# Landmark attention and an MLP on one core: the first weight matrix is cast on its way in, and the gain of the norm moves elsewhere

## The chip, the core and the metric

One core of a Trainium2 chip runs the kernel. TensorE (PE) multiplies matrices into PSUM; VectorE (DVE) and ScalarE (ACT) read PSUM and write SBUF; GpSimd (POOL) works from SBUF to SBUF; SyncE (SP) only starts transfers, which POOL and ACT also do, each from its own queue. 16 DMA engines, shared by all queues, move the data. The metric is device microseconds of one execution: the median of three runs of the kernel before is 260.62 us (260.29 to 260.78).

## The reference

Attention runs over batch 8, 8 heads, sequence 576, head dimension 64, with 32 landmarks: means of 18 rows of q or k. Three softmax matrices are formed, A from q and the landmarks of k, B from both kinds of landmarks, C from the landmarks of q and k. Z is an approximate inverse of B, found by six steps. Then follows a layer norm with gain `g_ln` and a two-layer MLP:

```
Z = B^T / (norm1(B) * norminf(B));  six times: Z = 2 Z - Z B Z
x = A Z C v                          # heads side by side: 576 x 512 for each batch
xn = (x - mean(x)) / std(x) * g_ln
out = x + relu(xn @ w_ch1) @ w_ch2   # w_ch1 is 512 x 2048, w_ch2 is 2048 x 512
```

## The kernel before, in words

The rows of x enter the MLP only through a short product. With Zc = Z C v (32 rows for each head), x is A times Zc, so `relu(xn @ W1)` is made from a small matrix m16 = Zc W1 (`psm`, then `m16`), and from A^T, kept as `ea`: `psh = m16^T ea`, `relu` writes `hT`, and W2 is applied to `hT`. The factor 1/std is positive and is applied at the very end, as `rstd`.

**W1, g and the mean.** `load_w1_0` to `load_w1_7`, all on SP, bring W1 as fp32 in eight pieces of 512 KB into the six staging buffers `stg`, which first hold q, k and v of batch 0; a piece waits until the cast that reads the buffer's former content is done. 16 operations `scale_w1_*` on POOL and ACT multiply by 16 g, row by row, and write the fp16 matrix `w1_16`. It has four column quarters f = 0 to 3. `less_mean_f*` (PE) multiplies a quarter by the constant matrix `lesser`, -1/512 everywhere; the result `less_f` is minus the column mean. For batches 0 and 1 the mean is taken off in `m16`: DVE computes less * zsum + psm. For the later batches `center_f*`, eight operations on DVE, adds `less_f` to W1 itself, so that `m16` is a plain copy. `zt_0` and `zt_1` are the transposed Zc of batches 0 and 1, copied from PSUM by `ztc_00`, `ztc_01` and `ztc_1`.

**W2.** It arrives as fp16 by four casting transfers on POOL's queue. Batches 0 and 1 use it plainly (`pso`); from batch 2 on, a scheme with seven half products takes the place of eight (`ps7a`, `ps7c`, `ps7e`) and uses differences of parts of W2 (`mix`) and of `hT` (`hmix`), made by POOL and DVE.

**Batches.** Batch 0 is loaded as fp32 by SP and cast by three engines; its transposes are made on PE (`turns_*`) and copied out of PSUM by `turned_*`. For the others q and k come as fp16 by casting transfers on POOL's queue into three buffers `nat`, v by SP into two buffers `vs`. Batch 1 is worked alone, batches 2 and 3, 4 and 5, 6 and 7 in pairs. The six steps are `step_*` (PE) and `next_*` (DVE or ACT) in turn. In the head of the kernel the chain is: cast of q and k, sums for the landmarks (`sums_*`), `qbd` and `klm`, `psb_0`, `expb_0`, `softmax_0`, `gram_*`, `scaled_0`, six steps, `zt_*`, `ztc_*`, `psm_01` (quarter 1 is taken first), `m16_01*`, `psh_0*`.

**The order.** There is no planner in the kernel: `ORDER` is a list of 1571 entries, a number and an engine letter each (P TensorE, D VectorE, A ScalarE, G GpSimd, S SyncE). The number names an operation, the letter the engine that does it. Every engine works through its own entries in this order, so one operation that waits holds back all that follow on its engine, transfers that this engine starts included. The first W1 piece stands seventh on SP after the loads of q, k and v. `warm_*` are 15 groups of matmuls on zeros whose results nobody reads.

Lines: 193 is every ordinary matmul, 197 the PE transposes, 200 copies and casts, 203 activations, 207 sums of two tensors, 210 the three-operand form, 223 every transfer, 357 the scaling of W1 on POOL, 1068 a relu on DVE, 1202 the making of g.

Of the kernel before, what the change touches and what calls it, by code (L numbers as in the profile page):

```python
# [19 lines left out]
0G 20P 23P 4S 12P 14P 24P 17P 11P 2S 1S 3S 6S 7S 10P 21P 28G 38P 25A 26D 34P 39D 40P 29P 30A 31P 27D  # L20
37P 32P 42D 41D 18P 33D 43P 65P 44A 45D 66A 61P 67P 46P 47P 250G 48D 22P 19P 15P 62A 68A 69A 71D
245G 49P 50D 63P 35P 13P 79G 80D 51P 52D 64A 36A 81P 70D 53P 72P 73A 5S 95S 54D 8P 9D 105A 106G 55P
56D 57P 74P 82D 260P 83D 58D 16P 84D 96S 59P 75A 76A 60D 85P 251D 86D 89P 90D 87P 88D 126P 261A 262D
108G 77G 94S 103G 93S 97S 101G 91D 92D 78D 107A 102G 127P 128P 129P 130A 167P 141P 142A 252P 253A
145P 169D 104A 168D 98S 254D 149P 150D 147P 148A 172P 173A 176P 247P 177A 248A 259D 255D 174P 175A
246D 256P 257A 146A 170P 171D 109G 110G 121P 122P 123P 111G 124P 268P 156P 258D 151D 249D 267P 112A
125A 275A 269A 270A 271A 157D 277A 158D 131P 132P 133P 134P 178P 163P 278D 279D 117G 273A 433G 274A
99S 113G 135A 180D 263S 164A 159P 280P 281D 160A 165P 166A 114G 264A 100S 115G 116G 265S 118G 136P
137P 266G 161P 179D 429G 119G 138P 139P 162D 282P 283D 140A 181P 182A 183P 284P 276D 285A 143P 187P
184D 286P 144A 188A 272D 152D 185P 186A 287D 297P 298D 299D 189P 191D 190D 288P 289A 294P 290P 295A  # L30
201P 202P 296A 300P 301A 291D 292P 293A 120G 455G 212P 213P 435G 436G 437G 310P 438G 445G 302A 303G
308P 309A 214P 330P 434D 444D 312D 311D 313D 332D 192P 193A 153D 154D 198P 199A 155A 441D 430D 439D
431D 331D 442D 440D 432D 443D 234P 556D 215P 304P 235P 236P 305A 306A 196P 446G 447G 203P 204P 194P
195A 237P 238P 205P 206P 451G 197A 307G 314P 315A 337P 339P 448G 449D 822G 338A 555D 239P 240P 241P
322P 207P 208P 574D 565D 569G 450D 340A 323A 216P 242D 209D 210S 217P 324D 341P 343D 223P 335P 244S
336A 342D 333P 463D 218P 219P 577G 452D 220D 344P 352P 353D 467G 468G 469G 470G 334A 826G 348P 345A
349A 346P 347A 457G 318P 319A 224P 316P 317A 225P 226P 227P 481P 458G 465D 459G 460G 482A 350P 454D
354D 357P 471D 464D 472D 351A 453D 363P 228P 229P 364D 358A 361P 230P 362A 461D 462D 365D 493P 494A
359P 368P 360A 483P 495P 355P 325D 326D 505A 369A 356A 231D 233A 200G 374P 375P 366P 367A 370P 371A
573G 506D 456D 507P 508P 509D 320P 321D 385P 484P 486A 487A 489A 510P 834D 511D 466D 491A 386P 387P  # L40
485A 388P 211S 512P 376P 473S 474G 490A 377P 496P 498A 501A 499A 497A 513D 514P 327D 488D 492D 328D
396P 397P 475S 476G 566G 828G 829G 830G 831G 572G 477S 478G 838G 839G 844G 564G 568G 503A 378P 379P
380P 515D 823D 502A 221S 504D 372P 516P 479S 480A 500D 517D 836D 528P 529P 530D 531D 398P 399P 373A
381P 522P 518P 389P 329A 866S 382D 418P 519D 824D 559D 520P 521D 523A 532P 419P 420P 524A 533A 534A
558D 550P 551D 552D 553D 548P 549A 421P 422P 423P 536P 424P 425P 848G 535G 832D 833D 554D 232S 867A
537A 538A 539G 560D 525P 527A 400P 401P 557D 426D 427S 605P 526A 606A 840G 841G 594P 595A 561D 540P
541A 390P 391P 611P 612A 837D 596D 827D 392P 393D 825D 850G 851G 852G 563D 603P 604A 853G 562D 859D
842D 860G 861G 843D 579P 613P 614A 407P 580A 601P 602A 609P 610A 1217G 585P 408P 845D 599P 409P 607P
600A 410P 411P 586A 597P 608A 542A 543G 856D 615P 598A 576G 626P 616A 412P 413P 581P 627A 402P 862G
394S 582A 570G 567D 617D 589D 835D 863G 858D 590D 618P 619A 634P 635A 643P 583P 584A 620P 621A 624P  # L50
414P 571G 874P 625A 622P 623A 628P 629A 644P 544P 847D 857D 545A 846D 591D 546A 875D 403P 632P 872S
633A 645P 630P 647P 592D 631A 646P 415D 877P 648P 649P 650P 864D 865D 854D 404D 855D 1191G 886P 638D
637G 641G 663P 664P 665P 639D 640D 662G 428S 417S 406S 661D 593A 882A 884A 879A 880A 883A 652D 878A
651D 657D 887A 889P 892A 896A 658D 666P 668D 894A 895A 849D 667D 653P 654P 711P 722P 712A 723A 891A
890A 655P 656P 547G 575G 675P 676P 677P 728P 729A 678P 695P 696A 1192D 713D 716P 881D 1194D 717A
724P 725A 876P 888P 1213G 660D 587P 870S 714P 416S 659D 871G 873G 384S 1229G 642G 1230G 1231G 726P
898A 715A 679D 682D 669P 897D 727A 588A 730P 222S 1232G 899D 900P 901P 731A 718P 732P 902D 743P 719D
578G 903P 904D 670P 720P 734A 733A 721D 744A 671P 672P 673D 699P 700A 893D 739P 636G 1203D 1239S
701P 905P 243S 741P 906D 740A 751P 674D 742A 703P 752A 907P 735P 736A 737P 383S 868S 681S 680S 683S
738A 702D 908D 909P 1219G 1195G 1220G 1221G 685P 704D 697P 698A 915P 917A 916A 910D 911P 1222G 759P  # L60
760P 749P 811P 925P 750A 761P 885D 869G 921P 926A 927A 753G 922P 1225D 755G 912D 913P 705D 706D 745P
746A 1227D 812P 707D 708D 709D 710A 813P 814P 747P 748A 686P 687P 688P 928G 929P 930A 1223D 1224D
1196D 1233D 815P 816P 923D 1228D 924D 914D 931A 1214D 943P 947D 944D 941P 817P 946D 945D 1240G 754G
756G 932G 758G 942A 762P 692D 767D 694S 689D 818P 763P 764P 918P 765P 766P 395S 1241S 1197G 920A
1198G 1199G 1200G 919A 819D 963P 974P 965A 975A 1207G 1208G 1209G 768D 769P 964D 774D 770P 956P 968P
1215D 1204D 957A 966P 690S 693S 405S 773D 969A 1226D 779P 967A 933P 934A 935A 780P 972P 948P 949A
1234D 1216D 970P 781P 973A 936G 984P 985A 820S 771P 971D 757D 986D 980P 772P 978P 782P 954P 776D
1242A 775D 981A 979A 976P 977A 955A 937P 1193D 938A 939A 1205D 785P 786P 787P 788P 982P 983A 1255P
989P 990A 1210G 684S 783D 1211D 1212D 1201D 1202D 1243P 777G 778G 784D 790D 691S 991P 1244A 789D
992A 801P 1235S 995P 996A 1245P 940G 1236G 1256D 1257P 802P 1267A 1268D 987P 988A 803P 993P 994A  # L70
1066P 1067D 804P 808D 1269P 1270P 1237S 1238G 1246P 1249A 805D 791P 792P 810S 1206D 1271D 821S 1248A
1247A 1253A 1250D 1251A 793P 958D 794P 1006G 1252A 809S 1003P 1004A 1272P 798D 1273D 997P 998A 950P
# [36 lines left out]
def kernel(  # L109
# [61 lines left out]
    def T(name):  # L171
        return handles[name]
# [1091 lines left out]
```

## Time and profile before

| | |
|---|---|
| median of three runs | 260.62 us |
| the profiled execution | 260.2 us, span 258.5 us |
| PE, DVE, ACT, POOL busy | 249.9, 212.3, 163.9, 177.5 us |
| read from HBM, written | 36.70 MB, 9.44 MB |

The span runs from the first to the last instruction; 1.7 us of the profiled execution's time lie around it. Busy PE is the time in which at least one matmul is in flight. Matmuls overlap, so that a row of eight with one duration may have been stretched by short waits that are no idle time. The granted TensorE clock was full in every part of the span.

### The profile page before, as it was taken

The page shows a single profiled execution, that of the slowest core. Times are in us where ns is not written, and L with a number is a line of the kernel's source. Part 1 is how long each engine was busy: PE and PEld are TensorE (multiplying, and loading weights), DVE is VectorE, ACT ScalarE, POOL GpSimd, SP SyncE. Part 2 cuts the span into 40 slices and gives each one's busy share as a digit, 9 for nine tenths or more (in the row PEclk, how much of TensorE's full clock was granted, in tenths as well). Part 3 has the DMA queues.
Part 4 walks back from the last instruction along what each step waited for, and adds up shares of the span by engine and source line. Part 5 has one row for each costly group of instructions (what it writes and reads, how often), then busy time and mean ns, then how long its engine had stood idle before and what let it go on. Part 6 is the DMA issues. An engine that isn't in the chain of part 4 may idle for free.

```text
span 258.5 us, 8351 instructions
## 1 busy us (share of the span) xinstructions
PE 249.9 (97%) x3499; PEld 179.8 (70%) x3499; DVE 212.3 (82%) x472; ACT 163.9 (63%) x304; POOL 177.5 (69%) x180
## 2 busy tenths in 40 slices
PE   7898999999999999999999999999999999999993
PEld 7766465556554557777766787777867787788981
DVE  1669899999999989997998869898547999878661
ACT  1588886747766999778756997868666245644000
POOL 8324899689794789699999995782078505966600
PEclk9999999999999999999999999999999999999999
DMA  6999999999749176949704832500130100510356
GB/s 234 367 269 338 374 210 208 207 235 244 227 127 178 29 164 87 221 89 286 140 4 121 231 93 61 127 3 3 41 85 0 44 20 9 115 23 20 82 121 184
DMA packets 23277, 36.32 MB, mean 140 GB/s; under 512 B 2116, under 2 KB 11592, under 8 KB 23240
## 3 DMA queue, kind: packets, MB, share of 16 engines
q1 hardware_dynamic: 12456, 23.37, 29.6%
q0 software_dynamic: 9504, 10.36, 25.1%
q10 hardware_dynamic: 1280, 2.07, 3.1%
q8 instruction: 27, 0.44, 0.7%
q14 instruction: 10, 0.08, 0.1%
HBM read 36.70 MB, written 9.44 MB: 178 GB/s over the span
## 4 chain that ended last, share of the span: by engine, by line
PE 85%; DMA 7%; ACT 3%; DVE 2%; issue 1%; SPq 1%; ACTq 0%; DVEq 0%
PE psh L193 23%; PE ps7a L193 16%; PE pso L193 15%; PE ps7c L193 8%; DMA w1s<-in_moe_w_ch_dram 5%; PE ps7e L193 4%; PE psm L193 3%; PE psy L193 3%; DMA stg_q<-in_q_dram 3%; PE it L193 2%; PE pscv L193 2%; PE psd L193 1%; PE psec L193 1%; PE psea L193 1%; PE pso_74a L193 1%
## 5 line engine op out<-in xcount | busy, mean ns | idle before, releaser
L203 ACT ACTIVATE hT<-psh 128x576 f16<-128x576 f32 x106 | 65.8, 650 | 30.4 <-PE psh L193 28.6
L193 PEld LDWEIGHTS <-hT 128*128 128x128 f16 x688 | 64.6, 98 | 22.6 <-issue 3.1
L193 PE MATMUL psh<-ea,m 128*128 128x288 f16 x512 | 78.2, 286 | 0.1
L193 PEld LDWEIGHTS <-m 128*128 128x128 f16 x512 | 48.9, 98 | 15.6 <-issue 1.3
L193 PE MATMUL pso<-w,hT 128*128 128x512 f16 x176 | 45.5, 380 | 0.0
L207 POOL TENSOR_TENSOR mix<-hT 128x1024 f16<-128x1024 f16 x8 | 17.0, 2125 | 27.4 <-ACT hT L203 27.4
L210 DVE SCALAR_TENSOR_TENSOR x<-ps7a,rstd,x 128x256 f32<-128x256 f32 x48 | 21.3, 477 | 6.7 <-PE ps7a L193 4.9
L193 PE MATMUL ps7a<-mix,hT 128*128 128x256 f16 x192 | 25.9, 273 | 0.0
L1068 DVE TENSOR_SCALAR hT<-psh 128x576 f16<-128x576 f32 x22 | 16.4, 753 | 10.1 <-PE psh L193 9.9
L997 DVE BATCH_NORM_STATS2 six<-x 128x6 f32<-128x512 f32 x36 | 24.2, 673 | 0.0
L207 POOL TENSOR_TENSOR ea<-ea,lns 128x576 f16<-128x576 f16 (+1 forms) x14 | 17.7, 1261 | 7.2 <-ACT lns L203 4.0
L200 ACT CAST m<-psm 128x512 f16<-128x512 f32 (+1 forms) x25 | 19.1, 793 | 4.5 <-PE psm L193 3.4
L200 ACT COPY x<-psy 128x512 f32<-128x512 f32 (+1 forms) x29 | 16.8, 587 | 7.6 <-PE psy L193 7.2
L193 PEld LDWEIGHTS <-mix 128*128 128x128 f16 x192 | 18.2, 98 | 4.3 <-issue 1.5
L207 POOL TENSOR_TENSOR mix<-mix,hT 128x1024 f16<-128x1024 f16 x8 | 16.9, 2124 | 6.2 <-DVE mix L207 5.8
L207 POOL TENSOR_TENSOR hT<-hT 128x1024 f16<-128x1024 f16 x9 | 19.1, 2123 | 0.2
L207 POOL TENSOR_TENSOR hT<-hT,mix 128x1024 f16<-128x1024 f16 x7 | 15.1, 2166 | 4.4 <-PE ps7e L193 2.5
L214 DVE TENSOR_REDUCE part<-xT_k 128x32 f16<-128x576 f16 x24 | 17.1, 737 | 0.0
L207 POOL TENSOR_TENSOR asum_q<-asum_q 128x256 f32<-128x256 f32 (+1 forms) x24 | 15.1, 628 | 1.5
L203 ACT ACTIVATE ec<-psec 128x256 f16<-128x256 f32 (+1 forms) x42 | 12.4, 428 | 5.3 <-PE psec L193 5.3
L193 PE MATMUL psy<-zcbd,ea 128*128 128x256 f16 x80 | 14.8, 273 | 0.2 <-ACT x L200 0.2
L200 POOL CAST natv<-stg_v 128x1152 f16<-128x1152 f32 (+1 forms) x12 | 13.8, 1163 | 1.4 <-DMA stg_v<-in_v_dram 1.3
(174 smaller groups left out, 471.2 us busy)
## 6 DMA issues: line engine op xcount, KB each, us to landing
out_dram<-x SPq DMA_DIRECT2D x55, 128.0 KB, 2.7
stg_v<-in_v_dram SPq DMA_DIRECT2D x10, 576.0 KB, 5.1
w1s<-in_moe_w_ch_dram SPq DMA_DIRECT2D x8, 512.0 KB, 11.6
nat_q<-in_q_dram POOLq DMA_DIRECT2D x7, 576.0 KB, 8.7
nat_k<-in_k_dram POOLq DMA_DIRECT2D x7, 576.0 KB, 7.5
w<-in_moe_w_ch_dram POOLq DMA_DIRECT2D x4, 512.0 KB, 8.5
out_dram<-x ACTq DMA_DIRECT2D x15, 128.0 KB, 2.4
stg_v<-in_v_dram SPq DMA_DIRECT2D x6, 288.0 KB, 4.5
```

The lines of the kernel that those rows point to most:

```text
L193: keep(nc.tensor.matmul(o, l, r, start=start, stop=stop, tile_position=(rb, cb), skip_group_check=(skip or cb != 0)))
L200: keep(nc.scalar.copy(o, i) if e == "A" else ENGINES[e].tensor_copy(out=o, in_=i))
L203: keep(nc.scalar.activation(*args, **kw))
L207: keep(ENGINES[e].tensor_tensor(out=o, in0=a, in1=b, op=f))
L210: keep(ENGINES[e].scalar_tensor_tensor(out=o, in0=a, scalar=s, in1=b, op0=f0, op1=f1))
L214: keep(nc.vector.tensor_reduce(out=o, in_=i, axis=axis, op=f))
L997: keep(nc.vector.bn_stats(out=T(f"six_{j}")[:], in_=T(f"x_{j}")[:]))
L1068: keep(nc.vector.tensor_scalar(out=o, in0=T(psh)[:, :, 0:HS], scalar1=0.0, scalar2=None, op0=ALU.max))
```

## The change

W1 comes by four casting transfers on POOL's queue (`load_w1_0` to `load_w1_3`, one for a column quarter) straight into `w1_16`, with no g in it. For batches 0 and 1 g is applied to `zt`: `ztc_00`, `ztc_01` and `ztc_1` become a multiplication on DVE. The matrix `lesser` becomes four matrices with -g/512 in them, made by one DVE operation from `g`, so that `less_f` is what it was. The 16 `scale_w1_*` stay, but work in place on fp16 and come after the last use of a quarter by batch 1, ahead of `center_*`, which POOL may now do as well.

Beside that, the cast of the second half of q of batch 0 is cut into two (DVE 5 of 9 parts, ACT the rest); the two `m16_01*` are cut into halves of 256 columns; the two loads of v of batch 1 may be started by ACT, and are. And `ORDER` is new as a whole. In it the head differs as follows. SP loads q00, k00, k01, q01, g, v00, v01 and then nothing for batch 1. POOL has the constants, `cast_k00`, `load_w1_1`, `load_q10`, `load_w1_0`, `load_k10`, `load_w1_2`, `cast_v00`, `cast_v01`, `norm_01_0`, `load_q20`, `norm_01_1`, `load_w1_3`, the four loads of W2, `load_k20`, `cast_v10`, `cast_v11`. ACT has `cast_k01`, `turned_k0`, the second part of `cast_q01`, `turned_k1`, `expb_0`, and starts v of batch 1 after `tot_q11` and after `x_02`. DVE has `turned_q1` between `softmax_0` and `scaled_0`, and `g` and `lesser` between `next_0_1` and `next_0_2`. PE has the four `less_mean_1*` ahead of `step_0_4`, both `total_q1*` ahead of `step_0_5`, and after `psm_01`: `less_mean_0*`, a warm group, `psh_005`, `psh_004`, `rows_02`, `total_k11`, `psh_007`, `total_k10`, `psh_006`, `psm_00`, `rows_04`, `psb_00`, `psec_00`, a warm group, `psm_02`. It is 622 entries long as before.

By engine over the whole list: six of the eight `center_*` go from DVE to POOL, the scales are 12 on ACT and 4 on POOL (4 and 12 before), `hmix_*` are 18 on DVE and 30 on POOL (16 and 32), casts of v are 5 on ACT and 11 on POOL (4, 11, and one on DVE), `relu_*` stay 22 on DVE and 106 on ACT. ACT starts 22 stores where it started 16. At the end PE takes the last block's 384 columns (`pso_74a`) before its 128 columns (`pso_74b`); before, it was the other way round. Two warm groups stand at the end of the list.

```
-        for i in range(8):
-            n = f"w1s_{i}"
-            buf(n, "stg", [P, 2, DM], FP32)
-            f, half = divmod(i, 2)
-            op(f"load_w1_{i}", "S", (n,),
-               lambda e, n=n, f=f, half=half: dma(
-                   e, T(n)[:], w1_src[:, 2 * half:2 * half + 2, ts(f, DM)]))
...
+        for f in range(4):
+            op(f"load_w1_{f}", "G", (),
+               lambda e, f=f: dma(e, w1_16[:, :, ts(f, DM)], w1_src[:, :, ts(f, DM)]))
...
-               lambda e, c=c: MM(T(f"psf_{f}")[:], lesser[:], w1_16[:, c, ts(f, 512)],
+               lambda e, c=c: MM(T(f"psf_{f}")[:], T("lesser")[:, c, :], w1_16[:, c, ts(f, 512)],
...
+            for c in range(KCH):
+                def scale(e, f=f, c=c):
+                    o = w1_16[:, c, ts(f, 512)]
+                    if e == "A":
+                        act(o, o, AF.Copy, scale=g_sb[:, c:c + 1])
+                    else:
+                        keep(ENGINES[e].tensor_scalar(out=o, in0=o, scalar1=g_sb[:, c:c + 1],
+                                                      scalar2=0.0, op0=ALU.mult, op1=ALU.add))
+                op(f"scale_w1_{f}{c}", "GAD", (), scale)
...
-                op(f"center_{f}{c}", "D", (f"less_{f}",), center)
+                op(f"center_{f}{c}", "DG", (f"less_{f}",), center)
...
-            op(f"ztc_0{w}", "AD", (f"pszt_0{w}", "zt_0"),
-               lambda e, w=w: copy(e, T("zt_0")[:, :, w, :], T(f"pszt_0{w}")[:, :, 0:LM]))
+            op(f"ztc_0{w}", "D", (f"pszt_0{w}", "zt_0"),
+               lambda e, w=w: tt("D", T("zt_0")[:, :, w, :], T(f"pszt_0{w}")[:, :, 0:LM],
+                                 g_sb[:, 2 * w:2 * w + 2, None].broadcast_to([P, 2, LM]), ALU.mult))
...
+    op("lesser", "D", ("lesser",), lambda e: keep(nc.vector.tensor_scalar(
+        out=T("lesser")[:], in0=g_sb[:, :, None].broadcast_to([P, KCH, P]), scalar1=-1.0 / DM, scalar2=None,
+        op0=ALU.mult)))
```

More of the change, by code (lines that the diff above doesn't have):

```diff
@@ L25 @@
[L25 to L29, printed above, removed]
@@ L924, in def_set @@
         op(zt, "P", (pszt, cv, st[6]), zt_)
[L925 to L926 removed]
+        if bs[0] <= LAST_WHOLE:
+            op(f"ztc_{s + 1}", "D", (pszt, zt),
+               lambda e: tt("D", T(zt)[:], T(pszt)[:, :, 0:W * LM].rearrange("p r (w l) -> p r w l", l=LM),
+                            g_sb[:].rearrange("p (u r) -> p r u", r=2)[:, :, :, None].broadcast_to([P, 2, W, LM]),
+                            ALU.mult))
+        else:
+            op(f"ztc_{s + 1}", "AD", (pszt, zt),
+               lambda e: copy(e, T(zt)[:].rearrange("p r w l -> p r (w l)"), T(pszt)[:, :, 0:W * LM]))
         def zc(e):
```

201 lines of the change are left out of this document (96 added, 105 removed).

## The prediction

> **What bounds the kernel now.** I read the page first, then busy time by stretches, then the chain of waits in the head. The page, and five stretches (us, length, then busy time and count of each engine, clock, DMA share, GB/s):
>
> ```profile
> span 258.5 us, 8351 instructions
> PE 249.9 (97%) x3499; PEld 179.8 (70%) x3499; DVE 212.3 (82%) x472; ACT 163.9 (63%) x304; POOL 177.5 (69%) x180
> ...
> 0.00:10.00 10.00, 8.16 (x101) 7.99 (x101) 3.18 (x11) 2.60 (x3) 6.29 (x29) 1.00 0.80 292
> 10.00:20.00 10.00, 8.70 (x247) 6.58 (x245) 7.17 (x25) 8.13 (x14) 2.85 (x4) 1.00 1.11 286
> 20.00:30.00 10.00, 9.35 (x127) 5.59 (x126) 8.93 (x22) 7.94 (x21) 6.66 (x10) 1.00 1.07 365
> 30.00:40.00 10.00, 9.67 (x145) 6.21 (x145) 9.63 (x26) 8.20 (x17) 9.18 (x13) 1.00 1.19 240
> 60.00:80.00 20.00, 20.00 (x393) 11.57 (x391) 18.68 (x45) 12.44 (x30) 17.27 (x20) 1.00 0.77 182
> 120.00:140.00 20.00, 20.00 (x401) 13.99 (x399) 18.12 (x44) 12.95 (x23) 19.62 (x17) 1.00 0.46 106
> 240.00:259.00 19.00, 14.15 (x130) 11.75 (x128) 8.81 (x21) 0.00 (x0) 4.20 (x2) 1.00 0.49 132
> ```
>
> PE is the bound: it is idle 258.5 - 249.9 = 8.6 us, of which 10.00 - 8.16, 1.30, 0.65 and 0.33, together 4.1 us, lie in the first 40 us and 4.8 in the last 19, where the row runs half a microsecond past the span. Between, rows like 60 to 80 and 120 to 140 show none. Only short stretchings, which a busy row hides, can be won there. So the change can pay in the head, at the end, or by those stretchings. The head's chain (start, us, what):
>
> ```profile
> 2.32 7.08 DMA stg_q<-in_q_dram
> ...
> 15.84 11.95 DMA w1s<-in_moe_w_ch_dram
> ...
> 27.81 0.73 ACT w L203
> ...
> 29.04 1.42 DVE m L210 x2
> ```
>
> The loads of q and k end at 9.40. Then, from 15.84 to 27.79, the chain is a W1 transfer: its cast-and-scale on ACT, `less`, two `m16` and the next `psh` follow. This is what the change touches.
>
> **The transfers.** Three stretches, with both kinds of loads, with plain ones alone, and with casting ones alone; then the start of k of batch 1 on POOL's queue (KB written, us to landing):
>
> ```profile
> 10.00:22.00 12.00, 10.51 (x261) 7.20 (x259) 9.13 (x33) 9.36 (x15) 4.00 (x5) 1.00 1.11 285
> 24.00:28.00 4.00, 4.00 (x68) 2.88 (x65) 3.60 (x7) 3.01 (x8) 2.82 (x5) 1.00 1.05 399
> 34.00:54.00 20.00, 19.83 (x230) 11.19 (x227) 19.66 (x42) 13.33 (x26) 16.71 (x21) 1.00 1.22 207
> ```
> ```profile
> nat_k<-in_k_dram POOLq DMA_DIRECT2D x1, 576.0 KB, 12.5
> ```
>
> Casting loads are counted by what they write, half of what they read: 207 GB/s is 414 read, beside 399 for plain ones. W1 reads the same 4 MB, so its transfers get no cheaper; only their order and what waits around them change. Before, k of batch 1 was started at 11.7 (POOL's rows below) and landed 12.5 us later, at 24.2. Up to then 8 MB had to come: batch 0's six loads, q and k of batch 1, half of W1. Afterwards the same 8 MB stand ahead of the landing of k, now with quarters 1 and 0 on POOL's queue: 512 + 576 + 512 + 576 KB written, 2.23 MB, or 10.8 us at 207 GB/s. POOL starts them from 7.6 on (its cast of k00 after the landing at 6.4, 1.14), 0.75 each, long before the engines are free. They flow alone from about 13, when v of batch 0 is through (two more loads of 590 KB at 399 GB/s after 9.40, slowed a little by sharing), less 0.2 MB that slip in earlier: k lands near 23.4. But ACT starts v of batch 1 after `tot_q11`, near 20, in the midst of this queue. When it begins to flow, near 21, k has 1.0 MB to read; with the first 0.59 MB of v at 399 GB/s k lands near 25.0 (at best 23.4; at worst 26.3, if all 1.18 MB of v goes first). W1's quarter 2 follows with 2.5 us: 25.9 without v, 28.9 with it.
>
> **The head on the engines.**
>
> ```profile
> 5.04 1.14 POOL L200 CAST nat_k<-stg_k 128x1152 f16<-128x1152 f32 x1 [0.33 <-DMA stg_k<-in_k_dram]
> 6.12 1.37 POOL L223 DMA_DIRECT2D nat_q<-in_q_dram  x1
> 11.73 0.75 POOL L223 DMA_DIRECT2D nat_k<-in_k_dram  x1 [4.24 <-PE it L193]
> ```
> ```profile
> 7.92 1.15 ACT L200 CAST nat_q<-stg_q 128x1152 f16<-128x1152 f32 x1 [5.83 <-DMA stg_q<-in_q_dram]
> 9.84 1.12 ACT L200 COPY xT_q<-pst_q 128x1152 f16<-128x1152 f16 x1 [0.77 <-PE pst_q L197]
> 11.62 0.21 ACT L203 ACTIVATE it<-it 128x64 f32<-128x64 f32 x1 [0.66 <-PE it L193]
> ```
> ```profile
> 6.41 0.76 DVE L200 CAST nat_k<-stg_k 128x1152 f16<-128x1152 f32 x1 [3.27 <-DMA stg_k<-in_k_dram]
> 13.24 0.22 DVE L214 TENSOR_REDUCE csum<-it 128x2 f32<-128x64 f32 x1 [0.40 <-PE it L193]
> 14.49 0.46 DVE L207 TENSOR_TENSOR ea<-ea,lns 128x288 f16<-128x288 f16 x1 [0.56 <-ACT lns L203]
> 15.06 0.76 DVE L200 CAST natv<-stg_v 128x1152 f16<-128x1152 f32 x1
> 19.42 0.22 DVE L210 SCALAR_TENSOR_TENSOR st<-st,it 128x64 f16<-128x64 f16 x1 [0.60 <-PE it L193]
> ```
> ```profile
> 22.83 0.81 PE L193 MATMUL psy<-zcbd,ea 128*128 128x256 f16 x6 [0.17 <-ACT x L200]
> 23.48 1.14 PE L193 MATMUL psh<-ea,m 128*128 128x288 f16 x8
> 24.46 0.67 PE L193 MATMUL psl_k<-nat_k,pairs 128*128 128x128 f16 x9
> 26.45 1.03 PE L193 MATMUL psf<-w,lesser 128*128 128x512 f16 x4
> 27.41 0.75 PE L193 MATMUL psec<-xT_k,lmt_q 32*32 32x288 f16 x32
> 30.03 0.88 PE L193 MATMUL psm<-w,zt 64*32 64x512 f16 x8
> ```
>
> *To the end of the steps: 0.4 us later.* The loads still land at about 5.0, 6.4, 7.9 and 9.4, when their casts began. ACT now has in a row the cast of k01 from 7.9 (1.15), `turned_k0` (1.12), 4 of 9 parts of the cast of q01 (0.5) and `turned_k1` (1.12): free for `expb_0` at 11.9, not 11.62, +0.3. `turned_q1` (0.76, as the cast of 1152 columns at 15.06) fills a DVE wait of 0.40 ahead of `scaled_0`: +0.35. In return `norm_00_1`, which waited 0.56 for ACT at 14.49, no longer stands before `next_0_0`: -0.5. `lesser` is new: 512 columns, no less than 512/1152 of that 0.76 (0.34), no more than 0.75, the line through the 0.35 for 128 and 0.62 for 384 columns of the last fence; I take 0.6, of which half falls in DVE's gap between two steps, +0.3. The multiplication in `ztc` instead of a copy: the same PSUM read, 0 (below 0.1). Four `less_mean` (0.96 from 26.45 to 27.41) and both `total_q1` (0.51 each, 24.46 to 24.97) delay the later steps, but are work of PE that had to come anyway. `next_0_5` starts at 19.85 for 19.42.
>
> *The first `psh`: 0.55 earlier.* Nothing scales W1 any more, so `less_1` is long done; `psm_01` still comes near 21.3, and `m16_01` needs only its first halves, each 0.43 (half of 1.42/2 is 0.36, and some of it is fixed), so `psh_005` starts at 22.9 for 23.48. What PE has done by then is alike: four `less_mean_0*` (0.96) in place of four `rows` (0.65 for three, 22.83 to 23.48).
>
> *k of batch 1: PE waits 0.9 us (0 to 2.2).* Two `psh` (0.98 for eight matmuls) and a `rows` (0.2) end at 24.1, and `total_k11` stands next, for a landing at 25.0. Behind it in PE's order stands everything.
>
> *Quarter 2: no more wait.* From 25.0 on come two totals (1.0), two `psh` (1.0), `psm_00` (0.4, as the row at 30.03 begins), `rows` (0.2), `psb`, a warm group (0.5 together) and `psec` (0.75), to 28.9, when quarter 2 lands. Before, `psm_02` ran at 30.03, 1.1 later, but by then four `less_mean_2*` (0.96) and two `rows` (0.43) were done that are still to come now. Net: the head is 1.4 - 1.1 = 0.3 us behind. Without the wait on k, and with quarter 2 at 25.9, `psm_02` runs at 28.0: 0.6 ahead. With k at 26.3 it is 1.6 behind, and 2.6 if POOL's queue also starts 1 us later.
>
> From there to 40 I take 0: quarter 3 now queues behind q of batch 2 and lands near 34.5, covered by eight `psh` (4 us, at 0.98 for two) and three steps that stand before its first use; should that cover fail, PE pays the rest.
>
> **The middle.** Nothing here is shown as idle time of PE. What moves, by groups:
>
> ```profile
> L207 DVE TENSOR_TENSOR w<-w,less 128x1024 f16<-128x1024 f16 x8 | 6.4, 816 | 0.0
> ```
> ```profile
> L207 POOL TENSOR_TENSOR hT<-hT 128x1024 f16<-128x1024 f16 x9 | 19.1, 2123 | 0.2
> L357 POOL TENSOR_SCALAR w<-w1s,g_sb 128x512 f16<-128x512 f32 x12 | 8.2, 693 | 9.4 <-DMA w1s<-in_moe_w_ch_dram 5.5 <-DVE g_sb L1202 3.9
> ```
> ```profile
> L203 ACT ACTIVATE w<-w1s,g_sb 128x512 f16<-128x512 f32 x4 | 2.9, 720 | 0.9 <-DMA w1s<-in_moe_w_ch_dram 0.9
> ```
>
> DVE loses six centers (4.9) and a cast of v (0.76), gains two sums of 1024 (0.8 each), `lesser` (0.6) and three split parts (below 0.2 each): about 3 us less, while it was busy 18.68 of 20 from 60 to 80. POOL gains six centers at its price for 1024 columns, 2.12 (12.7), and four starts at 0.75 (3.0), and loses two sums (4.2) and eight scales (5.5): 6 us more. ACT gains eight scales at 0.72 or less (5.8) and six store starts. All of it lies beside PE. Of DVE's 3 us I take 0.9 as paid on PE's path: the stretch rows show no idle PE, so most of it cannot be (0 to 2). That is the freest choice of the sum.
>
> The Trainium skill, "SBUF — State Buffer", section "SBUF: two separate sides", speaks against the change: while DVE copies or casts in its two-port mode, GpSimd cannot write the descriptors of its own transfers, and a plain load from SP would not care. The row agrees so far as it goes: the start at 6.12, across DVE's cast of 6.41, took 1.37 where the one at 11.73 took 0.75. By that rule the sum comes out at rival 3 below, without it at the forecast.
>
> **The end.** The last DVE operation and the one before:
>
> ```profile
> 252.57 0.35 DVE L210 SCALAR_TENSOR_TENSOR x<-pso_74b,rstd,x 128x128 f32<-128x128 f32 x1 [0.43 <-PE pso_74b L193]
> 254.19 0.62 DVE L210 SCALAR_TENSOR_TENSOR x<-pso_74a,rstd,x 128x384 f32<-128x384 f32 x1 [1.27 <-PE pso_74a L193]
> ```
>
> The last is now of 128 columns, 0.35 in place of 0.62: -0.3. Two warm groups now stand behind it, so nothing waits for them.
>
> **The sum.** +0.3 - 0.9 - 0.3 = -0.9 us. Against the profiled execution's own 260.2 (span 258.5 and 1.7 around it) that is 259.3; the median shown, 260.62, is 0.4 higher, so I forecast 259.7. A change under 0.2%, 0.5 us, can't be told from none.
>
> **Rivals.**
> (1) *The transfers come in time*: POOL's queue starts early enough, or v later than I think. PE does not wait for k: 0.6 + 0.9 + 0.3 = 1.8 us less, 258.8, and 257.7 with DVE's relief at its upper end. For it: 414 GB/s of casting loads alone beats the mixed stretch, where 285 were written. Against: k's load took 12.5 us to land.
> (2) *Slower: v of batch 1 cuts into POOL's queue.* The place is `total_k11` in PE's order. It decides where k lands after 26.0, past 1.9 us of waiting; at the bound the head loses 2.6, less 0.9 and 0.3: +1.4, 262.0; with no relief of DVE 262.9. For it: one queue now carries W1, q and k in order, where SP and POOL ran side by side at 11 to 24. Against: v needs `total_q11` first, which itself needs q.
> (3) *POOL's starts are held up by DVE.* The one that ran across DVE's cast of 6.41 took 0.6 more. A first start 0.6 later shifts k and quarter 2 by as much: with a second one lost ahead of k, 259.7 + 1.2 = 260.9. For it: the 1.37. Against: four of the five starts have a full queue ahead of them.
> (4) *POOL becomes the bound*: it is busy 19.62 of 20 from 120 to 140; its centers come before batch 2, and one sum of 2.12 late at a product there gives 261.8. Against: the stretch 60 to 80 leaves it 2.7 us.
> (5) *Nothing changes*: PE's list has the same 622 entries, and the head is hidden again by the rest: 260.6.
>
> **How the numbers follow.** Forecast 0.42, its own range 258.9 to 260.5 (0.34 faster, 0.08 same); rival 1 0.19, faster; 2 0.15, slower; 3 0.05, slower; 4 0.07 (0.05 slower, 0.02 same); 5 0.12, same. Faster 0.53, same 0.22, slower 0.25. The range 257.6 to 262.0 leaves out a tenth at either end: the far ends of rivals 1 and 2.
>
> **What would show it.** `total_k11` idle before it, released by the transfer, and k landing near 25; `psm_02` near 28.9; `psh_005` near 22.9; `next_0_5` near 19.85; the row 60 to 80 with less DVE and more POOL; a last DVE operation of 0.35. If PE's busy time in the first 40 us grows with no waits on k or quarter 2, rival 1 holds; if PE's idle time between 20 and 30 exceeds 2.5 us, rival 2. The forecast is wrong in kind if the time is gained or lost after 60 us by more than 2 us.

## The result: 263.7 us, slower by 1.2%

The changed kernel takes 263.7 us (median of 4 runs, 263.17 to 264.33); the kernel before, run beside it, takes 260.65 us (260.29 to 260.78). The ratio is 1.012, with a 95% interval of 1.0095 to 1.0145. The forecast was 259.7 us and its range ended at 262.0, so the time is outside of it, on the other side.

The profile after: the page's span and busy time, then stretches of it (us, length, then busy time and count of each engine, clock, DMA share, GB/s).

```profile
span 262.1 us, 8342 instructions
PE 251.4 (96%) x3499; PEld 181.3 (69%) x3499; DVE 216.5 (83%) x469; ACT 170.8 (65%) x314; POOL 181.8 (69%) x181
```
```profile
60.00:80.00 20.00, 20.00 (x391) 11.62 (x390) 18.97 (x45) 15.83 (x35) 17.95 (x16) 1.00 0.82 190
...
100.00:120.00 20.00, 17.52 (x253) 12.88 (x251) 19.50 (x32) 14.05 (x31) 12.85 (x14) 0.98 0.66 106
120.00:140.00 20.00, 18.88 (x377) 12.33 (x391) 15.25 (x39) 13.81 (x23) 10.23 (x12) 0.85 0.34 77
```

The place is the stretch from 100 to 140 us. Before, TensorE (the first number behind the length) was busy throughout, at clock 1.00; from 120 to 140 the prediction shows it, and this is the stretch ahead of that, before:

```profile
100.00:120.00 20.00, 20.00 (x304) 15.05 (x302) 18.41 (x42) 15.73 (x35) 17.47 (x14) 1.00 0.73 155
```

Now TensorE is idle for 2.5 and 1.1 us, and the clock of the second stretch is 0.85. A finer cut, and what TensorE waited for (us in total, times, longest):

```profile
112.00:116.00 4.00, 3.70 (x30) 2.78 (x29) 4.00 (x1) 3.68 (x8) 4.00 (x5) 1.00 1.00 150
116.00:118.00 2.00, 0.00 (x0) 0.00 (x0) 1.93 (x4) 0.39 (x1) 1.84 (x3) 1.00 0.00 0
118.00:120.00 2.00, 1.82 (x26) 1.01 (x25) 1.97 (x5) 0.64 (x1) 1.92 (x3) 0.83 0.00 0
120.00:122.00 2.00, 0.88 (x26) 0.39 (x32) 1.84 (x7) 0.66 (x2) 1.97 (x3) 0.50 0.31 9
122.00:124.00 2.00, 2.00 (x38) 1.02 (x23) 1.81 (x4) 1.50 (x2) 1.85 (x3) 0.50 0.93 141
```
```profile
PE it L193 <- DVE st L207: 3.5, 2, 2.4
```

TensorE waits twice for `st`, the result of `softmax_3` and then of `scaled_3` on VectorE. In 112 to 116 VectorE has one instruction and is busy all the time. The timeline of VectorE, then that of GpSimd (start, us, what):

```profile
111.69 5.62 DVE L207 TENSOR_TENSOR hT<-hT 128x1024 f16<-128x1024 f16 x1
117.24 0.28 DVE L214 TENSOR_REDUCE rsum<-it 128x4 f32<-128x128 f32 x1
```
```profile
110.42 0.74 POOL L223 DMA_DIRECT2D nat_q<-in_q_dram  x1 [4.44 <-DVE xT_q L220]
111.18 1.17 POOL L207 TENSOR_TENSOR mix<-w 128x512 f16<-128x512 f16 x1
112.29 1.16 POOL L207 TENSOR_TENSOR mix<-w,mix 128x512 f16<-128x512 f16 x1
113.39 2.26 POOL L200 CAST natv<-stg_v 128x1152 f16<-128x1152 f32 x2
115.61 1.14 POOL L207 TENSOR_TENSOR asum_q<-nat_q 128x512 f32<-128x512 f16 x1
116.83 1.60 POOL L207 TENSOR_TENSOR asum_q<-asum_q 128x256 f32<-128x256 f32 x2
```

One sum of two SBUF tensors, `hmix_224`, stands as 5.62 us; two such sums a few us earlier take 1.29 together. It ends at 117.31. GpSimd ran five instructions over the same time, each starting some 0.05 us before the recorded end of the one before it, and the first gap in that row is at 116.75 to 116.83, where `asum_q701` has to wait for the result of `asum_q700`. The sum's record ends 0.56 us behind the recorded end of `asum_q700`, a little less than the 0.64 us of one of the two plain sums; so all but the last part of the 5.62 is a wait for that gap. In the kernel before, `hmix_224` was one of GpSimd's own sums (2.11 us, at 116.64); the new order gave it to VectorE. Ahead of the five stands `load_q60`, a transfer that GpSimd starts, after 4.44 us of waiting for `turn_q50`.

### The profile page after: what moved, and what is told of

Read it like the earlier page. It is cut to its first block, busy times and chain, and to the rows that moved or that the text cites. A ratio compares the mean times of both kernels' runs of the same rounds, so it can differ in the third digit from the quotient of the medians.

```text
span 262.1 us, 8342 instructions
## 1 busy us (share of the span) xinstructions
PE 251.4 (96%) x3499; PEld 181.3 (69%) x3499; DVE 216.5 (83%) x469; ACT 170.8 (65%) x314; POOL 181.8 (69%) x181
## 4 chain that ended last, share of the span: by engine, by line
PE 81%; DMA 8%; DVE 6%; ACT 2%; issue 1%; SPq 0%; POOL 0%; ACTq 0%
PE psh L193 22%; PE ps7a L193 16%; PE pso L193 15%; PE ps7c L193 7%; DMA w<-in_moe_w_ch_dram 6%; PE ps7e L193 3%; PE psy L193 3%; PE psm L193 3%; DVE hT L207 3%; PE it L193 2%; DMA stg_k<-in_k_dram 2%; PE pscv L193 2%; DVE x L210 2%; PE psd L193 2%; PE psea L193 1%; PE pso_74a L193 1%
## 5 line engine op out<-in xcount | busy, mean ns | idle before, releaser
L203 ACT ACTIVATE hT<-psh 128x576 f16<-128x576 f32 x106 | 66.6, 652 | 36.1 <-PE psh L193 35.4
L193 PE MATMUL psh<-ea,m 128*128 128x288 f16 x512 | 79.7, 289 | 0.0
L193 PEld LDWEIGHTS <-m 128*128 128x128 f16 x512 | 49.4, 99 | 15.8 <-issue 1.7
L193 PE MATMUL pso<-w,hT 128*128 128x512 f16 x176 | 44.8, 380 | 0.0
L207 POOL TENSOR_TENSOR ea<-ea,lns 128x576 f16<-128x576 f16 (+1 forms) x14 | 16.9, 1208 | 27.5 <-ACT lns L203 25.0
L207 POOL TENSOR_TENSOR hT<-hT,mix 128x1024 f16<-128x1024 f16 x10 | 21.2, 2126 | 5.8 <-PE ps7e L193 3.3
L200 ACT CAST m<-psm 128x512 f16<-128x512 f32 (+1 forms) x27 | 20.0, 777 | 6.7 <-PE psm L193 5.8
L207 POOL TENSOR_TENSOR mix<-mix,hT 128x1024 f16<-128x1024 f16 x7 | 14.8, 2127 | 7.9 <-DVE mix L207 7.8
L200 ACT COPY x<-psy 128x512 f32<-128x512 f32 (+1 forms) x26 | 15.2, 584 | 2.0 <-PE psy L193 1.3
L207 POOL TENSOR_TENSOR asum_q<-asum_q 128x256 f32<-128x256 f32 (+1 forms) x24 | 14.5, 606 | 1.3
L207 POOL TENSOR_TENSOR mix<-hT 128x1024 f16<-128x1024 f16 x4 | 8.5, 2126 | 9.9 <-ACT hT L203 9.9
```

What stands on the lines that cost most here:

```text
L193: keep(nc.tensor.matmul(o, l, r, start=start, stop=stop, tile_position=(rb, cb), skip_group_check=(skip or cb != 0)))
L200: keep(nc.scalar.copy(o, i) if e == "A" else ENGINES[e].tensor_copy(out=o, in_=i))
L203: keep(nc.scalar.activation(*args, **kw))
L207: keep(ENGINES[e].tensor_tensor(out=o, in0=a, in1=b, op=f))
```

## The experiments

Theory T at the start: the sum is held while GpSimd runs instructions that read SBUF without a gap; TensorE idles behind it; the clock falls because of the idle time. Rivals: VectorE is simply too full in the new order (R1), the clock falls whatever TensorE does (R2), GpSimd is the full engine (R4). All names refer to the changed kernel.

### The clock: e1_fill

```
+    FILL = {"psh_307": 24, "psh_304": 10}
     for n, e in order:
         emit(n, e)
+        for i in range(FILL.get(n, 0)):
+            MM(T(n)[:, i % 2, HS:HS + 224], zeros[:, 0:P], zeros[:, 0:224], skip=True)
```

> The changed kernel with 34 matmuls of zeros put into TensorE's two waits (24 ahead of gram_a_3, 10 ahead of step_3_0, into columns of PSUM tiles that nothing reads); the computation is whole. Theory T (one VectorE sum, hmix_224, is held for 5.6 us while GpSimd runs five instructions that read SBUF without a gap; TensorE idles 2.4 + 1.1 us behind it, and the granted clock falls to 0.50 for some 7 us because of that idle time): the sum still takes about 5.6 us, softmax_3 still ends near 118, but the clock stays at 1.00 between 116 and 128 us and the kernel takes about 263.7 - 3.3 = 260.4 us. Rival R2 (the clock falls at this place whatever TensorE does, for instance from the load): it falls all the same and the time stays at 263.7 within 0.5.

Measured: 262.3 us (261.67 to 263.23), 1.0076 of before (1.0051 to 1.0101). The sum in this kernel, and two stretches:

```profile
112.25 5.62 DVE L207 TENSOR_TENSOR hT<-hT 128x1024 f16<-128x1024 f16 x1
```
```profile
116.00:120.00 4.00, 3.82 (x52) 3.27 (x50) 3.90 (x7) 0.83 (x3) 3.77 (x6) 1.00 0.04 7
120.00:126.00 6.00, 5.50 (x101) 3.96 (x100) 5.67 (x14) 4.43 (x7) 4.68 (x6) 1.00 0.70 111
```

The sum is as long as it was, to the hundredth, and the clock stays at 1.00: it fell because of the idle time, and R2 is out. But the gain is not 3.3 us. The span is 260.6 for 262.1, 1.5 less, and this execution reached the sum 0.56 us later (112.25 for 111.69), so by these two traces the low clock cost about 2.1 us. The 3.3 was half of the nearly 7 us at low clock, as if TensorE had set the pace in all of it; at full clock it still idles 0.18 + 0.50 us there.

### The sum on another engine, or later: e2_pool, e4_later

```
-... 642D ...          # hmix_224 on VectorE
+... 642G ...          # e2_pool: on GpSimd, at its place
```
```
-... 885D 642D 899D 1225D ... 902D 378S ...
+... 885D 899D 1225D ... 902D 642D 378S ...   # e4_later: behind scaled_3 (902)
```

> The changed kernel with one letter of the order changed: hmix_224 is issued on GpSimd at its place, not on VectorE. Theory T: VectorE goes from ecT_22 straight to softmax_3, whose first instruction starts near 111.8 instead of 117.2; TensorE's waits of 2.4 and 1.1 us and the low clock go, so 263.7 - 3.5 - 3.3 = about 257 us (256.3 to 258.5); GpSimd pays some 2 us later in its stream. Rival R1 (VectorE is overloaded in this order, the long record is only how its lateness shows): 0.7 us less work on VectorE gives at most 0.7 us, 263 or more. Rival R4 (GpSimd is the engine that is full): its stream gets 2 us longer and what follows is later by it, 264 or more.

> The changed kernel with hmix_224 moved behind scaled_3 in VectorE's own queue; its only reader, seven_24_04, comes later still. Each engine has the work it had. Theory T: softmax_3 and scaled_3 read PSUM and are not held; they end by about 114.5, and the sum then waits out what is left of GpSimd's stretch (to 116.75) or runs beside its end: at most 2.5 us, behind which next_3_0 waits; about 257 to 258.5 us with the clock at 1.00. Rival R1 (VectorE overloaded): the work is the same, the gain at most the 0.7 us of the sum, 263 or more.

Measured: e2_pool 259.34 us (259.08 to 259.73), 0.9962 of before (0.9948 to 0.9976); e4_later 258.47 us (258.12 to 258.83), 0.9926 (0.9911 to 0.9942). In e4_later, on VectorE:

```profile
113.12 0.29 DVE L214 TENSOR_REDUCE rsum<-it 128x4 f32<-128x128 f32 x1 [0.71 <-ACT it L203]
...
117.47 0.68 DVE L207 TENSOR_TENSOR hT<-hT 128x1024 f16<-128x1024 f16 x1
```

Moving one entry of the list gains 5 us, with the same work on every engine, and VectorE even has 0.71 us to spare ahead of `softmax_3`. R1 is out. So is R4: e2_pool gives GpSimd more work and is 4.4 us faster than the changed kernel. The sum, started at the moment of GpSimd's gap, takes its plain 0.68. e2_pool gains less, and misses the expected 256.3 to 258.5, because GpSimd needs 2.12 us for the sum and TensorE then waits for that, at a place where it did not:

```profile
PE ps7a L193 <- POOL hT L207: 1.5, 1, 1.5
```

These 1.5 us of idle time did not move the clock (1.00 in the stretch).

### A shorter row of GpSimd's instructions: e3_casts_early

```
-... 1213G 1195G 675P 676P 677P 573G 577G 869G 873G 1219G ...
+... 1213G 869G 873G 1195G 675P 676P 677P 573G 577G 1219G ...
```

> The changed kernel with cast_v41 and cast_v51 moved up in GpSimd's queue, ahead of load_q60, so that they run in its 4.4 us of waiting (105.98 to 110.42) and no longer stand in the stretch beside hmix_224; VectorE's queue is as it was. Theory T: the stretch of GpSimd's instructions is 2.26 us shorter and so is the sum, about 3.4 us instead of 5.6; TensorE waits 1.2 us instead of 3.5; with that little idle time the clock holds: 263.7 - 2.3 - 3.3 = about 258 us; if the clock falls all the same, 261.4. Rival R1 (VectorE overloaded): the same work in the same order on VectorE, 263.7 within 0.5.

Measured: 263.16 us (262.12 to 264.71), 1.0111 of before (1.0069 to 1.0153): nothing gained. VectorE in this kernel:

```profile
107.62 2.28 DVE L207 TENSOR_TENSOR mix<-mix,hT 128x1024 f16<-128x1024 f16 x1
...
114.42 3.41 DVE L207 TENSOR_TENSOR hT<-hT 128x1024 f16<-128x1024 f16 x1
```

The duration came out at 3.41 for a forecast of 3.4, and the time did not, because the two casts, now behind `load_k70`, held another sum as well (2.28 for 0.69), for which TensorE waited 1.0 us. It still waited 2.1 us for `st`, and the clock still fell, from 121.9 on for 3.4 us; besides, in this execution it waited 1.2 us for k in the head, where the edit changes nothing. By its time alone this run would fit R1 too; the two durations do not. The hold goes where the row goes. It also shows that T is not yet complete: from 107.62 on, the sum was not let in between the two casts either.

### A gap early in the row: e5_gap

```
-... 1213G 1195G 675P 676P 677P 573G 577G 869G 873G 1219G 1220G ...
+... 1213G 1195G 1219G 1220G 675P 676P 677P 573G 577G 869G 873G ...
```

> The changed kernel with asum_q700 and asum_q701 moved up in GpSimd's queue, from behind cast_v51 to directly behind load_q60. The same five instructions stand beside hmix_224, which stays where it was in VectorE's queue; but the second of them now is asum_q701, which reads what asum_q700 writes and so leaves a gap of some 0.08 us (as at 116.75 to 116.83 in the trace of the changed kernel). Theory T, now in a sharper form (VectorE's sum gets its turn only where GpSimd's next instruction has to wait for the one before; between independent ones it gets none): the sum starts at about 111.7 and gets in near 112.35, so it takes 1.2 to 1.4 us; TensorE's waits and the low clock go; 258.3 to 259.3 us. Rival (the sum waits until the whole bunch is done, or a fixed number of instructions): 5 us or more for the sum, 263 to 264.

Measured: 257.59 us (257.47 to 257.78), 0.9886 of before (0.9867 to 0.9904), the fastest of all, and below the expected 258.3 to 259.3. VectorE, then GpSimd:

```profile
111.78 1.20 DVE L207 TENSOR_TENSOR hT<-hT 128x1024 f16<-128x1024 f16 x1
```
```profile
111.25 1.17 POOL L207 TENSOR_TENSOR asum_q<-nat_q 128x512 f32<-128x512 f16 x1
112.50 1.06 POOL L207 TENSOR_TENSOR asum_q<-asum_q 128x256 f32<-128x256 f32 x1
```

Only GpSimd's queue was reordered, with the same five instructions beside the sum. The gap now lies at 112.42 to 112.50, and the sum gets in there. The hold thus cost 262.1 - 255.9 = 6.2 us of span: about 2.1 by the clock, 3.5 by the two waits, and 0.6 that no run separates.

### The hold by itself: e6_hold, e10_start, e11_pause

Three small kernels with nothing but GpSimd rows of five or six instructions beside one VectorE instruction. The core of e10_start, cut down; e11_pause is built alike:

```
def stretch(stream, n, before=None):
    keep(nc.gpsimd.memset(do[:, 0:16], 0.0))          # the marks
    keep(nc.gpsimd.memset(lead[:, 0:16], 0.0))
    if before: before()                               # a transfer started by GpSimd or by SyncE, or none
    stream()                                          # six casts or sums on GpSimd
    for i in range(n):                                # VectorE: n reads of PSUM ...
        keep(nc.vector.tensor_copy(out=lead[:], in_=acc[:]))
    keep(nc.vector.tensor_tensor(out=do[:], in0=da[:], in1=db[:], op=ALU.add))   # ... then the sum
```

> This kernel leaves the whole computation out and writes zeros; it measures the hold by itself. Six VectorE instructions (a sum of two SBUF tensors, a copy fp16 to fp16, a cast from SBUF fp32, a cast from PSUM, the three-operand form with PSUM and SBUF, the three-operand form with two SBUF tensors), each alone and beside three GpSimd streams of five instructions: independent sums, sums of which each reads the result of the one before, independent casts. Theory T: the sum takes 0.68 us alone, 5 to 6 us beside five independent sums or casts of 1.1 us each, and at most about 1.8 beside the dependent ones; both forms that read PSUM keep their time within 0.1 us beside every stream; the three-operand form with two SBUF tensors is held like the sum; of the copy and the cast from SBUF no row of the kernel tells, and they may go either way. Rival (the long record is not a hold by GpSimd but DMA traffic or an artefact of the profile): all keep their time in every stream, for there is no traffic here.

> This kernel leaves the whole computation out and writes zeros. In the measurement of the hold by itself VectorE got in after one GpSimd instruction, independent or not, so theory T in its sharper form has fallen there; in the kernel the sum was passed over by four boundaries in a row, and both stretches in which that happened (111.7 in the changed kernel, 107.6 and 114.4 in the one with the casts moved) begin with a transfer that GpSimd starts. Theory S: after GpSimd has started a transfer of its own, its next instructions follow without letting VectorE in, until one has to wait for the one before. It expects: streams without a transfer hold the sum for one instruction at most (1.7 us or less); six casts or sums behind a transfer started by GpSimd hold it through all that are left, 4 to 6 us; with a dependent cast as the fourth, to the third's end, 2 to 3 us; a transfer started by SyncE changes nothing. Rival M: what matters is whether VectorE arrives in the first instruction of a stream or in a later one; then the sums that arrive behind three or four reads of PSUM are held long with or without a transfer, and those that arrive early are not.

> This kernel leaves the whole computation out and writes zeros; nine stretches, each twice, of GpSimd starting a transfer and running six casts beside a VectorE instruction. Theory S (a transfer that GpSimd starts makes its next instructions follow without letting VectorE in, until one has to wait for the one before) expects: with a dependent cast second, a sum that arrives later, in the third or fourth, is held for one instruction only if the pause ends the state (1.7 us or less), or to the end (3 us or more) if a pause helps only while VectorE is already there; the same question for two tiny dependent copies between the transfer and the casts and for a wait of 4 us; a tiny independent memset between them changes nothing (5 us or more); two casts, a transfer and four casts with the sum arriving ahead of the transfer: held to the end of the first or second cast. A copy and a cast from SBUF and the three-operand form with two SBUF tensors are held like the sum (5 us or more). Rival: only the sum is held so, the three others get in after one cast.

e6_hold contradicted theory T: beside five independent casts the sum was let in after the first of them.

```profile
88.66 1.67 DVE L57 TENSOR_TENSOR do<-da,db 128x1024 f16<-128x1024 f16 x1 [4.77 <-POOL do L79]
```

The difference to the kernel had to lie elsewhere, and in the kernel every row that held a sum for long began with a transfer started by GpSimd. That is theory S, which e10_start tests. VectorE there: no transfer; a transfer ahead of casts (arriving in the first, then in a later one), ahead of sums, ahead of casts with a dependent one as the fourth; last, a transfer started by SyncE:

```profile
22.19 1.10 DVE L79 TENSOR_TENSOR do<-da,db 128x1024 f16<-128x1024 f16 x1
...
37.38 6.61 DVE L79 TENSOR_TENSOR do<-da,db 128x1024 f16<-128x1024 f16 x1
...
47.09 5.38 DVE L79 TENSOR_TENSOR do<-da,db 128x1024 f16<-128x1024 f16 x1
...
54.12 6.94 DVE L79 TENSOR_TENSOR do<-da,db 128x1024 f16<-128x1024 f16 x1
...
62.70 3.61 DVE L79 TENSOR_TENSOR do<-da,db 128x1024 f16<-128x1024 f16 x1
...
70.24 0.99 DVE L79 TENSOR_TENSOR do<-da,db 128x1024 f16<-128x1024 f16 x1
```

Which sums are held, and up to where, is as S expects. Three of the durations lie above its figures (6.61 and 6.94 for at most 6, 3.61 for at most 3), because the sum arrived in the first instruction and the row itself is that long: six casts take 6.58 us, six sums 6.68, three casts 3.32. In the row with the dependent cast the sum still ends right behind the third. Rival M is out, since a sum that arrived late in a row without a transfer took 0.68, and 1.71 in the second pass. e11_pause then asked what ends the state. In order: a dependent cast ahead of the sum's arrival; a tiny memset between transfer and casts; two tiny dependent copies between them; last, a tiny copy of an older result, so one whose wait is already over:

```profile
18.52 1.17 DVE L72 TENSOR_TENSOR do<-da,db 128x1024 f16<-128x1024 f16 x1
...
25.43 6.51 DVE L72 TENSOR_TENSOR do<-da,db 128x1024 f16<-128x1024 f16 x1
...
34.31 1.07 DVE L72 TENSOR_TENSOR do<-da,db 128x1024 f16<-128x1024 f16 x1
...
50.07 6.61 DVE L72 TENSOR_TENSOR do<-da,db 128x1024 f16<-128x1024 f16 x1
```

So a real pause, in which GpSimd waits for its own result, ends it for all that follows; an instruction alone does not. (That last stretch was meant to hold GpSimd for 4 us, but VectorE's reads ran ahead of it; what a long wait does was not tried.) Where the transfer came third, behind two casts, and the sum ahead of it, the sum got in after the first cast (0.99). Three other VectorE forms that read SBUF are held in the same way behind a transfer: a copy of fp16 and a cast from fp32 6.58 us each, the three-operand form with two SBUF tensors 7.38. Not every such form is: beside GpSimd's row behind `load_k70` in the kernel before (112.49 to 119.44) a reduction and a transpose that read SBUF keep 0.71 and 0.50. Forms that read PSUM are not held: the cast keeps 0.69 and the three-operand form 0.41 to 0.42 beside every row of e6_hold.

### The cure in the kernel: e12_pair

```
         emit(n, e)
+        if n == "load_q60":
+            keep(nc.gpsimd.tensor_copy(out=tiny[1][:], in_=tiny[0][:]))
+            keep(nc.gpsimd.tensor_copy(out=tiny[2][:], in_=tiny[1][:]))
```

> The changed kernel with two tiny copies on GpSimd, of which the second reads what the first writes, put in directly behind load_q60 (and one memset of 16 columns among the constants); every other instruction and its place is as it was. If a pause ends the state that the transfer's start brings (theory S, first form), hmix_224 is held for mix_24 only, about 0.7 to 1.4 us long, TensorE's waits and the low clock go and the kernel takes 257.5 to 258.5 us. If a pause helps only while VectorE is already waiting, the sum stays at 5.4 to 5.7 us and the time at 263 to 264.

Measured: 258.04 us (257.64 to 258.59), 0.9898 of before (0.9861 to 0.9935). VectorE, then GpSimd:

```profile
112.00 1.58 DVE L207 TENSOR_TENSOR hT<-hT 128x1024 f16<-128x1024 f16 x1
```
```profile
111.46 0.21 POOL L1239 COPY tiny<-tiny 128x16 f16<-128x16 f16 x1
111.73 0.20 POOL L1240 COPY tiny<-tiny 128x16 f16<-128x16 f16 x1
111.89 1.15 POOL L207 TENSOR_TENSOR mix<-w 128x512 f16<-128x512 f16 x1
```

The sum takes 1.58 for an expected 0.7 to 1.4, held by `mix_24` alone. 0.4 us of idle work on GpSimd gains 5.7 us of the kernel, and apart from a memset among the constants no other instruction was touched. With this the cause is shown, not argued.

### The priced steps: e7_centers, b1_centers_pool, e8_v_early

The three edits are told in words, since each touches several entries of the order:

```
-               six center_* on GpSimd (letters G)
+ e7_centers: the changed kernel with hmix_224 behind scaled_3 and these six on VectorE (D)
+ b1_centers_pool: the kernel before with the same six on GpSimd (G instead of D)
+ e8_v_early: the changed kernel with hmix_224 behind scaled_3; load_v10, load_v11 on SyncE, behind load_v01
```

> The changed kernel with hmix_224 behind scaled_3 (as in the run that moved it there, 258.47 us) and with the six center operations of GpSimd given back to VectorE at their places in the list, as they were before the change. If the step of the prediction holds that VectorE's relief pays 0.9 us on TensorE's path, this takes about 259.4 us; if GpSimd is the fuller engine, 258 or less; if neither is on the path, 258.5 within 0.3.

> The kernel before with one part of the change alone: six of the eight center operations are given to GpSimd at their places in the list, the same six as in the change. The step of the prediction that prices VectorE's relief at 0.9 us (0 to 2) expects 260.5 - 0.9 = 259.6 us; rival 4 of the prediction (GpSimd becomes the bound) expects a product that waits for a late sum of GpSimd, 261 or more. By the run that gave the six back to VectorE in the changed kernel and lost 5.4 us up to batch 2, the gain may be up to that size, but only if the kernel before were as short of VectorE at these places, and its stretches show no idle TensorE there.

> The changed kernel with hmix_224 behind scaled_3 and with the two loads of v of batch 1 started by SyncE directly after those of batch 0, near 4.5 us, in place of ScalarE's starts near 19.5 and 24. By the prediction's account of the transfers their 1.18 MB then stand ahead of GpSimd's queue: k of batch 1 and quarter 2 of W1 land 2.4 to 2.9 us later, total_k11 waits that much longer, and the kernel takes 258.5 + 2.5 = about 261 us. If the engines serve GpSimd's queue first, or the head has that much slack, 258.5 to 259.5.

Measured: e7_centers 264.45 us (264.0 to 265.14), 1.015 of before (1.0127 to 1.0173); b1_centers_pool 268.51 us (267.82 to 269.57), 1.0318 (1.029 to 1.0346); e8_v_early 264.47 us (263.66 to 265.19), 1.0148 (1.012 to 1.0175). Two stretches of e7_centers, and a wait of TensorE in b1_centers_pool:

```profile
40.00:60.00 20.00, 17.67 (x126) 10.13 (x119) 19.69 (x33) 16.24 (x30) 16.27 (x21) 1.00 1.06 206
60.00:80.00 20.00, 18.27 (x321) 10.43 (x319) 19.52 (x45) 14.71 (x32) 10.48 (x12) 1.00 0.82 175
```
```profile
PE psm L193 <- POOL w L207: 4.8, 1, 4.8
```

Given back to VectorE, the six centers cost 6 us (264.45 against 258.47), far outside of all that was expected: TensorE idles 2.3 and 1.7 us in these two stretches. Given to GpSimd in the order of before, they cost 8 us, of which 4.8 are one product of TensorE that waits for a late center. The assignment and the order belong together; neither has a price by itself, and "0.9 us of relief" was the wrong kind of term. In e8_v_early k of batch 1 was started at 11.72 and landed 15.8 us later, at 27.5. Its row, two waits of TensorE and a stretch:

```profile
nat_k<-in_k_dram POOLq DMA_DIRECT2D x1, 576.0 KB, 15.8
```
```profile
PE psf L193 <- DMA w<-in_moe_w_ch_dram: 1.9, 1, 1.9
PE psl_q L193 <- DMA nat_q<-in_q_dram: 1.5, 1, 1.5
```
```profile
20.00:30.00 10.00, 7.91 (x83) 4.57 (x82) 4.10 (x14) 1.81 (x4) 4.91 (x7) 0.56 1.23 207
```

So v ahead of GpSimd's queue does delay that queue, by 3.6 us for k. The loss is larger than the 2.5 of the expectation: TensorE already waits for W1 and q, before k, and the clock falls at 21.3, in the second of these waits; its mean between 20 and 30 us is 0.56.

## Why the prediction was wrong, step by step

- **The middle** is the step that failed. It took 0.9 us of gain there and gave as its bounds 0 to 2, because "nothing here is shown as idle time of PE". That no wait stands in a profile does not mean that a new order makes none. It priced the sums that VectorE gains as two of 0.8 us, the balance of 12 that the order gives to VectorE and 10 that it gives to GpSimd. One of the 12, `hmix_224`, took 5.62, because it stands beside a row of GpSimd that begins with `load_q60`; in the trace of before no VectorE sum of two SBUF tensors of this size falls into such a row. The price is 6.2 us of span: 262.1 against 255.9 in e5_gap. The prediction's own sign of being wrong in kind, more than 2 us lost after 60 us, is what happened.
- **Rival 3** had the right two engines and the wrong direction: VectorE holding up GpSimd's starts. The starts at 7.22 and 8.90 did take 0.93 and 0.95 for 0.75, and nothing came of it. What cost was a start of GpSimd holding up VectorE, at 111 us. The Trainium skill, "SBUF — State Buffer", section "Who interferes with whom", has the contention in both directions: a VectorE instruction with two SBUF inputs and a GpSimd instruction that reads SBUF exclude each other, and whichever is first keeps the port for its whole instruction. Without a transfer the runs agree (1.10 and 1.67, one instruction of GpSimd); behind a transfer they do not (6.61, six instructions), and there the measurement decides. No part of the prediction asked which VectorE sums the new order lays beside which GpSimd rows.
- **Rival 2** named the side on which the time fell, slower, but its place, `total_k11`, is not where it was lost.
- **"DVE loses about 3 us".** The whole kernel's VectorE time without the hold is 211.9 us (e5_gap's page), for 212.3 before: 0.4 less, and not 3. The six centers went (5.2 us), but three copies of x more (2.0) and costlier sums came, which the count by groups had left out. The row 60 to 80 has 18.97 where less than 18.68 was expected.
- **The head** was better than its step. This is `psh_005`, `total_k11` and `psm_02` of the changed kernel, and how long the transfers of k (batches 1 and 2) and of v (batch 1, started at 19.5 and 23.8) took to land:

```profile
22.44 1.14 PE L193 MATMUL psh<-ea,m 128*128 128x288 f16 x8
23.42 0.38 PE L193 MATMUL psy<-zcbd,ea 128*128 128x256 f16 x2
23.91 0.68 PE L193 MATMUL psl_k<-nat_k,pairs 128*128 128x128 f16 x9
...
28.20 0.41 PE L193 MATMUL psm<-w,zt 64*32 64x512 f16 x8 [0.37 <-DMA w<-in_moe_w_ch_dram]
```
```profile
DMA to landing us min/median/max: 12.9/17.4/21.9
```
```profile
DMA to landing us min/median/max: 7.9/8.1/8.3
```

  The first `psh` came at 22.44 (22.9 expected). k, started at 11.00, landed at 23.9 and not at 25.0, so TensorE waited 0.1 us for it instead of 0.9. The transfer of v did not take half of the engines: started at 19.5, it landed 8.3 us later, at 27.8, behind k. Quarter 2 came near 28.2 (28.9 expected). By the prediction's own bookkeeping (1.39 us of work still to come) the head is 1.39 - (30.03 - 28.20) = -0.4 us, not +0.3: nearly the 0.6 of rival 1.
- **The end** was right: the last VectorE operation takes 0.35 for 0.62.

```profile
258.34 0.35 DVE L210 SCALAR_TENSOR_TENSOR x<-pso_74b,rstd,x 128x128 f32<-128x128 f32 x1 [0.28 <-PE pso_74b L193]
```

- **The sum** without the hold: the span falls from 258.5 to 255.9, by 2.6: -0.4 in the head, -0.3 at the end, and so -1.9 in between, the upper end of the 0 to 2. Where in the middle these 1.9 us lie was not separated. TensorE is busy 247.8 us in e5_gap for 249.9 before, with as many matmuls, which points at shorter stretchings rather than shorter waits; VectorE's 0.4 us less in all do not explain them. The change without the hold gives 257.6 to 258.0 (e5_gap, e12_pair), at the low end of the range and about 2 us faster than the forecast, and one place in the order turned it into 263.7.

## What to carry to other kernels

Before a new order is trusted, list the VectorE instructions that take two inputs (or copy) from SBUF and the GpSimd rows beside them, above all rows that begin with a transfer which GpSimd starts: such a row held a sum to its first real pause. The cure here was a pause right behind the start (two tiny dependent copies, 0.4 us) or a dependent pair placed first in the row; moving instructions out of the row only moved the hold (e3_casts_early). And an instruction that lasts many times its usual duration may be a wait, as it was here: look at what another engine was doing at its end, not at its start.

## What the runs showed of the hardware

- Behind a transfer started by GpSimd, six instructions in a row kept a VectorE sum that arrived in the first or second of them out for 5.37 to 6.94 us; without one, or behind one of SyncE, a sum got in after one instruction at most (0.68 to 1.71). Two tiny dependent copies ended the state (1.07), a memset (6.51) and a copy whose wait was over (6.61) did not. Why the start has this effect, no run here shows.
- In the changed kernel the clock fell behind one gap of 2.41 us: the mean of 0.83 from 118 to 120 puts the fall near 119.3, ahead of the second gap, and the low clock cost about 2.1 us. The length of a single gap does not decide it: one of 1.5 us in e2_pool did not move the clock, but in e3_casts_early, where the longest is 1.5 us too, it fell at 121.9. There TensorE is idle for 2.1 us in all from 118 to 122, in e2_pool for 1.5. The low stretches last 6.83 us in the changed kernel, 3.41 in e3_casts_early and in b1_centers_pool (behind a gap of 4.8) and 10.24 in e8_v_early, all multiples of 3.41. What exactly decides was not tried. The Trainium skill, "TensorE: Matmul & The Clock Gate", section "HAM oscillation — how this bites in real kernels", gives as the rule no idle gaps above about 3.4 us; here shorter ones were enough, so waits of 1.5 us already have to be looked at where others stand beside them.
